# A windowed-attention and feed-forward kernel: the weight loads are begun by GpSimd's queue in place of SP's

## The chip, the cores and the metric

The kernel runs on one core of a Trainium2 chip. The metric is the device time of one execution in microseconds; the kernel before takes 941.67 us, the median of three runs (940.76 to 941.94). Engines are named as in the profile: PE (matmul), DVE (VectorE), ACT (ScalarE), POOL (GpSimd) and SP (the engine whose queue begins transfers).

## The reference

For 8 batches, 8 heads, 576 positions and 64 numbers per head, attention looks back over a window: heads 0 to 3 see the last 32 positions, heads 4 to 7 every fourth of the last 128. The heads side by side give rows of 512, which go through a norm and a feed-forward block with a residual.

```python
scores = scale * np.matmul(q, k.transpose(0, 1, 3, 2))
scores = np.where(masks[None, :, :, :], scores, -1000000000.0)
attn = np.exp(scores - np.max(scores, axis=-1, keepdims=True))
attn_out = np.matmul(attn / (np.sum(attn, axis=-1, keepdims=True) + 1e-09), v)
x = attn_out.transpose(0, 2, 1, 3).reshape(B, S, H * D)          # (8, 576, 512)
xn = (x - mean) / np.sqrt(var + 1e-06) * g_ln
out = x + np.maximum(xn @ w_ch1, 0.0) @ w_ch2                    # 512 -> 2048 -> 512
```

The two weight matrices come in as 64-bit numbers (8.4 MB each).

## The kernel before

The 4608 rows are 36 tiles of 128, taken three to a block. Each tile goes through attention (scores, softmax, values), the norm, two DMA transposes into `xT` (`transposes`, L576), the up matmuls (L597, 2048 hidden numbers in four groups of 512) and the down matmuls (L620). Every fp32 operand of the feed-forward block is held as two fp16 halves, so a product is three matmuls.

**The weights** are read once, at the start. `to_f32` (L645) loads a piece of 1 MB into a tile named `slot` (for the first column group of w1 two pieces of 0.5 MB), turns the 64-bit numbers into fp32 with one ACT operation (L659) and three DVE operations (L661, L662, L666), and lets PE sum the absolute values (L673). There are 18 such loads: four of 0.5 MB and six of 1 MB for w1 (`prep_w1`), eight of 1 MB for w2 (`load_w2`). When a whole column group of w1 is in, its scale is found (`scale_of`, L680) and the group is split into halves (`split_w1`, L153 on ACT and L154 on DVE). w2 has one scale, known only when the last load is summed; then `split_w2` splits it in eight steps, here called P0 to P7, and the down matmuls can begin, tile by tile.

**Slots.** The `slot` tiles share five buffers. They hold the weight pieces, the values of the first four tiles, the keys and queries of every second later tile, and the split keys of each tile. A load into a slot waits until the slot's previous user is done.

**Tiles 0 to 3** (`EARLY`) run in fp32 (`scores_early` and the like) between the weight loads. From tile 4 on, `load_tile_now` loads keys and queries (L186), `prep_stacked` splits them on ACT and POOL (L308, L279, L309, L280). Each group of nine tiles needs a scale for its values, found in `scale_v`: nine loads of a 256 KB row tile (L225, two buffers, shared with other tiles of that name), each squared by ACT (L226), then a sum on DVE (L228) and a matmul on PE (L230).

**What sets the order.** The pieces of work are units with a due time (`TIMES`, `MOVED`), emitted in order of that time; then the framework's scheduler places the instructions of each engine in one fixed order by its own model of their durations, and every engine and queue works its list in order. All transfers are begun by SP, so a transfer that must wait for a buffer holds up all transfers behind it. One more rule sits beside the weights: `state["raw"]` keeps the last weight load, and the loads of tiles 0 to 5 are emitted inside `tc.issue_after(raw)` (`after_weights`, L161), which puts instructions of that load's own engine behind it.

Of the kernel before, what the change touches and what calls it, by code (L numbers as in the profile page):

```python
# [68 lines left out]
def attention_then_ffn(ctx: ExitStack, tc, qkv, masks, g, w1, w2, out):  # L69
    nc = tc.nc  # L70
# [88 lines left out]
    state = {}  # L159
# [90 lines left out]
    def slot():  # L250

        return work.tile([P, CW * DM * 2], I32, name="slot", bufs=SLOTS)
# [392 lines left out]
    def to_f32(src, dst, ps, weights, start, stop, first=False):  # L645

        nw = len(weights)
        raw = slot().rearrange("p (a c two) -> p a c two", a=nw, two=2)  # L650
        src = src.rearrange("(a p) c two -> p a c two", p=P)
        step = 1 if first else nw
        for a in range(0, nw, step):
            on = slice(a, a + step)
            state["raw"] = nc.sync.dma_start(out=raw[:, on], in_=src[:, on]).ins
            lo, hi, at = raw[:, on, :, 0], raw[:, on, :, 1], dst[:, on]


            nc.scalar.activation(at, hi.bitcast(F32), AF.Abs, scale=2.0**-112)  # L659
            mi = at.bitcast(I32)  # L660
            nc.vector.tensor_scalar(mi, mi, scalar1=3, scalar2=None, op0=ALU.logical_shift_left)  # L661
            nc.vector.scalar_tensor_tensor(  # L662
                out=lo, in0=lo, scalar=29, in1=mi, op0=ALU.logical_shift_right, op1=ALU.bitwise_or
            )

            nc.vector.scalar_tensor_tensor(  # L666
                out=mi, in0=hi, scalar=SIGN_BIT, in1=lo, op0=ALU.bitwise_and, op1=ALU.bitwise_or
            )

        up = raw.bitcast(BF16).rearrange("p a c two -> p a (c two)").rearrange("p a (c four) -> p a c four", four=4)[:, :, :, 1]  # L670
        for a in range(nw):
            for c in range(0, DM, SUMS):
                nc.tensor.matmul(  # L673
                    ps[:, 0:SUMS], weights[a], up[:, a, c : c + SUMS],
                    start=start and a == 0 and c == 0, stop=stop and a == nw - 1 and c == DM - SUMS,
                )
# [13 lines left out]
    def prep_w1(fg):  # L690
        if fg == 0:
            nc.scalar.activation(g_abs, g_sb, AF.Abs)
        fs = slice(fg * DM, (fg + 1) * DM)
        wf = w1_sb[:, fg + 1]
        ps = ps_f.tile([P, DM], F32, name="ps_f")
        for c in range(0, NKC, CW):
            to_f32(
                w1[c * P : (c + CW) * P, fs], wf[:, c : c + CW], ps,
                [repeated(g_abs[:, c + a : c + a + 1]) for a in range(CW)],
                c == 0, c == NKC - CW, fg == 0,  # L700
            )
        s1.append(scale_of(ps, T_W1, f"s1_{fg}"))
# [8 lines left out]
    def load_w2(f):  # L711
        if f == 0:
            state["w2_ps"] = ps_f.tile([P, DM], F32, name="ps_f")
        to_f32(
            w2[f * P : (f + CW) * P, :], w2_f32(f, CW), state["w2_ps"], [repeated(s1[f // 4][:, 1:2])] * CW,
            f == 0, f == NFC - CW,
        )
# [195 lines left out]
```

## Time and profile before

| | |
|---|---|
| median of three runs | 941.67 us |
| profiled execution, its own time | 944.02 us |
| its span, first to last instruction | 942.2 us |
| granted TensorE clock, mean over the span | 0.985 |
| PE busy | 890.7 us |
| PE idle | 51.5 us, most of it in the first 140 us |

The profile lists, per engine, when each instruction ran, what ended the idle time before it, and when a transfer's data arrived. The span is cut into stretches below; a stretch's row gives each engine's busy time in it.

### The profile page before, as it was taken

The numbers are of one execution on the slowest core, as the hardware profiler recorded it, in microseconds if no ns is written. First come the engines' busy times: TensorE is split into PE (matmuls) and PEld (weight loads), VectorE is DVE, ScalarE is ACT, GpSimd is POOL, SyncE is SP. The second block draws the span as 40 slices with busy tenths as digits, with TensorE's granted clock in tenths as the row PEclk, the third lists the DMA queues.
The fourth block names the chain that finished last, engine by engine and source line by source line (L and its number), as shares of the span: only waits on it lengthen the run. The fifth ranks groups of instructions, "written<-read, shape, count | busy, mean of one in ns | idle before, by whom it ended". The sixth has DMA issues, their size and how long they took to land.

```text
span 942.2 us, 18610 instructions
## 1 busy us (share of the span) xinstructions
PE 890.7 (95%) x7608; PEld 552.2 (59%) x7608; DVE 634.2 (67%) x1379; ACT 312.7 (33%) x588; POOL 312.3 (33%) x319
## 2 busy tenths in 40 slices
PE   4479789999999999999999999999999999999998
PEld 4379466777665555565565565565565565564553
DVE  4799658896977577786686686686686685660210
ACT  4556742334323343251241451241241341130110
POOL 1010273646234235454253353354243341120000
PEclk9979899999999999999999999999999999999999
DMA  7887872754344516446143654364043411010000
GB/s 241 311 229 229 187 176 50 153 122 115 66 75 93 148 52 133 92 71 136 37 80 71 169 105 71 89 123 90 30 88 69 87 27 37 21 24 23 12 1 34
DMA packets 79622, 93.39 MB, mean 99 GB/s; under 512 B 47920, under 2 KB 53680, under 8 KB 79536
## 3 DMA queue, kind: packets, MB, share of 16 engines
q1 hardware_dynamic: 79536, 92.21, 42.3%
q8 instruction: 59, 0.97, 0.4%
q14 instruction: 27, 0.22, 0.1%
HBM read 71.86 MB, written 9.44 MB: 86 GB/s over the span
## 4 chain that ended last, share of the span: by engine, by line
PE 81%; DMA 10%; ACT 3%; DVE 3%; issue 2%; SPq 1%; POOL 1%; ACTq 0%; DVEq 0%; POOLq 0%
PE ps_f L597 36%; PE ps_f L620 35%; PE ps_s L330 4%; PE ps_v L528 4%; DMA row<-in_qkv 4%; DMA slot<-in_w 3%; DMA xT<-xl 1%; ACT row L226 1%; DMA slot<-in_qkv 1%; DMA v<-in_qkv 0%; PE ps_f L673 0%; ACT w_sb L153 0%; DVE slot L662 0%; POOL slot L280 0%; DVE slot L154 0%
## 5 line engine op out<-in xcount | busy, mean ns | idle before, releaser
L620 PE MATMUL ps_f<-w_sb,hh 128*128 128x512 f16 x1152 | 345.0, 380 | 5.8 <-ACT w_sb L153 5.0
L597 PEld LDWEIGHTS <-w_sb 128*128 128x128 f16 x3072 | 256.0, 99 | 126.6 <-issue 4.6
L620 PE MATMUL ps_f<-w_sb,hl 128*128 128x512 f16 x576 | 219.1, 380 | 0.0
L597 PE MATMUL ps_f<-xT,w_sb 128*128 128x384 f16 (+1 forms) x1536 | 199.2, 289 | 2.9 <-DMA xT<-xh 2.4
L597 PE MATMUL ps_f<-w_sb 128*128 128x384 f16 (+1 forms) x1536 | 196.7, 287 | 0.0
L620 PEld LDWEIGHTS <-hh 128*128 128x128 f16 x1152 | 111.8, 98 | 131.5 <-issue 6.8
L603 ACT ACTIVATE hh<-ps_f 128x384 f16<-128x384 f32 (+1 forms) x184 | 91.1, 500 | 216.8 <-PE ps_f L597 216.8
L604 DVE SCALAR_TENSOR_TENSOR hl<-ps_f,hh 128x384 f16<-128x384 f32 (+1 forms) x184 | 100.2, 569 | 42.4 <-ACT hh L603 40.3
L620 PEld LDWEIGHTS <-hl 128*128 128x128 f16 x576 | 56.5, 98 | 67.1 <-issue 1.8
L362 DVE TENSOR_TENSOR sc<-ps_s,mask 32x256 f32<-32x256 f32 x128 | 53.6, 419 | 51.2 <-PE ps_s L330 49.8
L435 DVE STREAM_TRANSPOSE pt_d<-pk 32x256 f32<-32x256 f32 x128 | 79.4, 621 | 1.8
L626 DVE SCALAR_TENSOR_TENSOR row<-ps_f,s,x 128x512 f32<-128x512 f32 x36 | 27.0, 749 | 74.5 <-PE ps_f L620 74.0
L446 POOL TENSOR_TENSOR sc<-sc,mx 128x512 f32<-128x512 f32 x32 | 33.4, 1043 | 116.3 <-DVE mx L444 116.3
L451 ACT ACTIVATE p<-sc 128x512 f32<-128x512 f32 x32 | 20.2, 631 | 128.2 <-POOL sc L446 128.2
L569 POOL TENSOR_TENSOR xl<-xn,xh 128x512 f16<-128x512 f32 x36 | 42.0, 1166 | 59.1 <-ACT xh L568 49.8
L330 PE MATMUL ps_s<-slot 128*128 128x128 f16 (+1 forms) x768 | 58.8, 226 | 2.1 <-DVE sc L348 2.1
L330 PEld LDWEIGHTS <-slot 128*128 128x128 f16 x768 | 50.9, 99 | 12.7 <-DVE sc L348 3.0
L287 POOL COPY slot<-slot 128x128 f16<-128x128 f16 x56 | 17.5, 340 | 119.4 <-PE ps_v L528 119.3
L348 DVE TENSOR_TENSOR sc<-ps_s,mask 32x256 f32<-32x256 f32 x128 | 53.5, 418 | 4.9 <-PE ps_s L330 3.4
L453 POOL TENSOR_TENSOR pk<-p,pk 128x512 f16<-128x512 f32 x32 | 40.7, 1271 | 45.8 <-ACT pk L452 45.8
L458 DVE STREAM_TRANSPOSE pt_b<-pk 32x128 f16<-32x128 f16 x87 | 26.1, 300 | 42.0 <-ACT pk L452 28.4
L554 POOL TENSOR_TENSOR rstd<-rstd,mhalf 128x1 f32<-128x1 f32 x36 | 21.1, 587 | 94.9 <-DVE rstd L553 85.2
(100 smaller groups left out, 961.3 us busy)
## 6 DMA issues: line engine op xcount, KB each, us to landing
qk<-in_qkv SPq DMA_DIRECT2D x36, 512.0 KB, 6.9
slot<-in_qkv SPq DMA_DIRECT2D x32, 512.0 KB, 6.7
slot<-in_w SPq DMA_DIRECT2D x14, 1024.0 KB, 6.3
out_x<-row SPq DMA_DIRECT2D x36, 256.0 KB, 2.0
row<-in_qkv SPq DMA_DIRECT2D x33, 256.0 KB, 2.9
v<-in_qkv SPq DMA_DIRECT2D x33, 256.0 KB, 3.0
slot<-in_w SPq DMA_DIRECT2D x4, 512.0 KB, 7.3
slot<-in_qkv SPq DMA_DIRECT2D x28, 64.0 KB, 4.5
```

The source lines that it names most:

```text
L330: nc.tensor.matmul(out, lhs, rhs, start=(n == 0), stop=(n == len(terms) - 1))
L348: nc.vector.tensor_tensor(out=sc[pj, 0:HP, :], in0=ps[pj, :, W * j : W * j + 2 * W], in1=mask_16[pj, m : m + 1, :].broadcast_to([W, HP, 2 ...
L362: nc.vector.tensor_tensor(out=sc[pj, HP:H, :].rearrange("p h (t i) -> p h t i", t=2), in0=ps[pj].rearrange("p h (t c) -> p h t c", t=2)[:, ...
L435: nc.vector.transpose(dd[pj].rearrange("p t h (i r) -> p r t h i", r=DIL)[:, j], pk[pj, HP:H, :].rearrange("p h (t i) -> p t h i", t=2),)
L446: nc.gpsimd.tensor_tensor(out=sm, in0=sc, in1=mx.broadcast_to([P, H, 2 * W]), op=ALU.subtract)
L453: nc.gpsimd.tensor_tensor(out=pk16[:, :, :, 1], in0=p32, in1=pk16[:, :, :, 0], op=ALU.subtract)
L528: nc.tensor.matmul(oo, l, r, start=(n == 0), stop=(n == len(mm) - 1))
L569: nc.gpsimd.tensor_tensor(out=xl, in0=xn, in1=xh, op=ALU.subtract)
L597: nc.tensor.matmul(z[:, n], l, r, start=(m == 0), stop=(m == len(mm) - 1))
L603: nc.scalar.activation(hh, z, AF.Relu)
L604: nc.vector.scalar_tensor_tensor(out=hl, in0=z, scalar=0.0, in1=hh, op0=ALU.max, op1=ALU.subtract)
L620: nc.tensor.matmul(o, l, r, start=(f == 0 and m == 0), stop=(f == NFC - 1 and m == 2))
```

## The change

The weight loads are begun by POOL's queue; nothing else in the text changes.

```diff
@@ -652,7 +652,7 @@
         step = 1 if first else nw
         for a in range(0, nw, step):
             on = slice(a, a + step)
-            state["raw"] = nc.sync.dma_start(out=raw[:, on], in_=src[:, on]).ins
+            state["raw"] = nc.gpsimd.dma_start(out=raw[:, on], in_=src[:, on]).ins
             lo, hi, at = raw[:, on, :, 0], raw[:, on, :, 1], dst[:, on]
```

The rule of `issue_after` names the engine of the weight load. With the load on POOL it holds back only the POOL instructions of the tile loads (memsets), and no longer SP's transfers; and the scheduler places everything anew in the first part of the program. From about the third block on the orders are the same. Three places, as the programs list them.

SP's queue at the start, the rows behind the mask's load: before, and then with the change. `in_w` are the weights, `qk_103` keys and queries of an early tile, `slot<-in_qkv` values of tiles 0 and 1, `row<-in_qkv` the rows of the values' scale, `v_1332` and `v_1428` the values of tiles 4 and 3.

```order
L655 DMA slot<-in_w 128x1024 x4
L213 DMA slot<-in_qkv 32x3x128
L213 DMA slot<-in_qkv 32x4x128 x2
L213 DMA slot<-in_qkv 32x3x128
L213 DMA slot<-in_qkv 32x4x128 x2
L175 DMA qk_103<-in_qkv 128x1024
L213 DMA slot<-in_qkv 32x4x128 x8
L655 DMA slot<-in_w 128x2x1024 x2
L225 DMA row<-in_qkv 128x512 x2
```

```order
L175 DMA qk_103<-in_qkv 128x1024
L225 DMA row<-in_qkv 128x512
L194 DMA v_1332<-in_qkv 128x512
L293 DMA v_1428<-in_qkv 128x512
L225 DMA row<-in_qkv 128x512
L213 DMA slot<-in_qkv 32x4x128 x3
L213 DMA slot<-in_qkv 32x3x128
L213 DMA slot<-in_qkv 32x4x128 x2
L213 DMA slot<-in_qkv 32x3x128
L213 DMA slot<-in_qkv 32x4x128 x7
```

The weights are gone from SP, tile 1's keys and the values of tiles 3 and 4 are loaded first of all (before, the latter came behind the last weight load), and tile 0's values come behind a row load that waits for a buffer.

POOL's queue with the change, from the first weight load to the last; before, the same rows stood there without L655. `mask_80` is the mask that tile 0's scores need, `rstd` and `xl` belong to the norms of tiles 0 and 1.

```order
L655 DMA slot<-in_w 128x1024 x4
L203 MEMSET slot 128x8x2
L655 DMA slot<-in_w 128x2x1024
L203 MEMSET slot 128x8x2
L740 CAST mask_80<-row 128x384
L655 DMA slot<-in_w 128x2x1024 x5
L203 MEMSET slot 128x8x2
L655 DMA slot<-in_w 128x2x1024
L554 TENSOR_TENSOR rstd<-rstd,mhalf 128x1
L655 DMA slot<-in_w 128x2x1024
L569 TENSOR_TENSOR xl<-xn,xh 128x512
L655 DMA slot<-in_w 128x2x1024
```

```order
L203 MEMSET slot 128x8x2
L554 TENSOR_TENSOR rstd<-rstd,mhalf 128x1
L655 DMA slot<-in_w 128x2x1024 x2
L569 TENSOR_TENSOR xl<-xn,xh 128x512
L655 DMA slot<-in_w 128x2x1024 x3
```

Five loads now stand ahead of the mask's cast, and the last seven alternate with the norms of tiles 0 and 1.

ACT's queue around the splitting of w2: before, and then with the change. `w_sb<-w_sb,s_...` are the steps P0 to P7, `row,v_sums` the squared rows, `slot<-qk_1329` the keys and queries of tile 4, `pk` the exponentials of tile 3.

```order
L413 ACTIVATE pk<-ps_s,less 128x64 x8
L603 ACTIVATE hh<-ps_f 128x4x128
L153 ACTIVATE w_sb<-w_sb,s_2_1539 128x2x512
L308 CAST slot<-qk_1329 128x1024
L279 CAST slot<-qk_1329 128x4x128
L279 CAST slot<-qk_1329 128x512
L226 ACTIVATE row,v_sums<-row 128x512 x2
L153 ACTIVATE w_sb<-w_sb,s_2_1539 128x2x512
L153 ACTIVATE w_sb<-w_sb,s_3_1541 128x2x512
```

```order
L413 ACTIVATE pk<-ps_s,less 128x64 x8
L153 ACTIVATE w_sb<-w_sb,s_0_1535 128x2x512 x2
L226 ACTIVATE row,v_sums<-row 128x512
L561 ACTIVATE xn<-x,shift,rstd 128x512
L603 ACTIVATE hh<-ps_f 128x4x128
L423 COPY pt_a_81<-ps_s 128x256
L425 COPY pt_d_85<-ps_s 128x64 x4
L308 CAST slot<-qk_1329 128x1024
L279 CAST slot<-qk_1329 128x4x128
L279 CAST slot<-qk_1329 128x512
L226 ACTIVATE row,v_sums<-row 128x512
L153 ACTIVATE w_sb<-w_sb,s_1_1537 128x2x512
```

Before, five of the eight steps stand ahead of tile 4's keys; now only P0 and P1 do. On PE the order follows: ahead of the matmul L230 that closes the scale for tiles 9 to 17, the program before has 72 down matmuls (L620), 19 up matmuls of block 1 (L597) and 8 score matmuls of tile 4 (L330); with the change 54, none and 24. Ahead of the first L620, both have 384 L597.

## Rows read from the trace of the kernel before

**Rows 1.** The page: the span, the engines' busy time, and the 40 equal slices (23.6 us each) with PE's busy tenths.

```profile
span 942.2 us, 18610 instructions
PE 890.7 (95%) x7608; PEld 552.2 (59%) x7608; DVE 634.2 (67%) x1379; ACT 312.7 (33%) x588; POOL 312.3 (33%) x319
...
PE   4479789999999999999999999999999999999998
```

**Rows 2.** Busy time of each engine (and count of instructions) in stretches of 20 us, then granted clock, DMA share and GB/s.

```profile
0.00:20.00 20.00, 7.74 (x128) 6.19 (x130) 8.22 (x20) 7.26 (x20) 3.93 (x20) 1.00 0.74 217
20.00:40.00 20.00, 9.30 (x159) 8.06 (x159) 14.08 (x23) 9.00 (x16) 0.12 (x1) 1.00 0.97 360
40.00:60.00 20.00, 11.76 (x110) 10.54 (x110) 17.84 (x34) 14.19 (x31) 3.51 (x3) 0.77 0.90 240
60.00:80.00 20.00, 19.23 (x345) 18.48 (x344) 19.99 (x35) 10.46 (x14) 2.16 (x2) 0.89 0.87 225
80.00:100.00 20.00, 18.84 (x382) 18.17 (x380) 17.68 (x39) 12.90 (x31) 1.71 (x2) 1.00 0.53 190
100.00:120.00 20.00, 15.39 (x66) 7.09 (x66) 10.88 (x11) 16.19 (x34) 7.23 (x5) 0.83 0.94 201
120.00:140.00 20.00, 15.39 (x208) 13.00 (x206) 10.01 (x27) 10.11 (x22) 13.40 (x15) 0.91 0.72 168
```

**Rows 3.** The weight loads as a group (line L655): ns that SP spends on one issue (least, median, most) with the first and last start, and us from issue to landing.

```profile
L655 SPq DMA_DIRECT2D slot<-in_w x18: 368/390/942, 2.1 to 82.7; - x18
...
DMA to landing us min/median/max: 4.8/6.8/13.2
```

**Rows 4.** Waits of SP's own queue between 0 and 150 us: total us, times, longest.

```profile
SPq L225 <- ACT row L226: 15.7, 10, 6.6
SPq L213 <- DMA slot<-in_w: 11.1, 7, 3.3
```

**Rows 5.** The timeline of 0 to 40 us: start, us, engine, line; in brackets the idle time before it and what ended it.

```profile
2.12 1.87 SPq L655 DMA_DIRECT2D slot<-in_w  x4
...
2.93 0.97 POOL L202 MEMSET slot<- 128x1040 f32 x1
...
8.62 0.66 ACT L659 ACTIVATE w_sb<-slot 128x512 f32<-128x512 f32 x1 [6.01 <-DMA slot<-in_w]
...
17.69 1.51 SPq L655 DMA_DIRECT2D slot<-in_w  x2
...
23.24 1.12 ACT L659 ACTIVATE w_sb<-slot 128x1024 f32<-128x1024 f32 x1 [1.21 <-DMA slot<-in_w]
...
28.74 0.90 SPq L655 DMA_DIRECT2D slot<-in_w  x2
...
38.79 1.12 ACT L659 ACTIVATE w_sb<-slot 128x1024 f32<-128x1024 f32 x1 [6.59 <-DMA slot<-in_w]
...
39.95 0.69 DVE L661 TENSOR_SCALAR w_sb<-w_sb 128x1024 int32<-128x1024 int32 x1 [3.48 <-ACT w_sb L659]
```

**Rows 6.** The timeline where tile 0's norm ends and the first up matmuls begin.

```profile
50.08 1.47 POOL L569 TENSOR_TENSOR xl<-xn,xh 128x512 f16<-128x512 f32 x1 [7.69 <-ACT xh L568]
...
58.75 5.17 PE L597 MATMUL ps_f<-xT,w_sb 128*128 128x128 f16 x47 [0.18 <-DMA xT<-xl]
```

**Rows 7.** The timeline of the last weight loads and of SP behind them.

```profile
78.05 4.97 SPq L655 DMA_DIRECT2D slot<-in_w  x2
...
85.56 1.13 ACT L659 ACTIVATE w_sb<-slot 128x1024 f32<-128x1024 f32 x1 [1.65 <-DMA slot<-in_w]
...
89.94 1.17 ACT L659 ACTIVATE w_sb<-slot 128x1024 f32<-128x1024 f32 x1
...
91.75 3.16 SPq L247 DMA_DIRECT2D v_b<-vh  x4
...
96.70 0.89 SPq L225 DMA_DIRECT2D row<-in_qkv  x2
```

**Rows 8.** The timeline from the first step of w2's splitting to L230.

```profile
102.69 2.17 ACT L153 ACTIVATE w_sb<-w_sb,s 128x1024 f16<-128x1024 f32 x2
...
103.24 1.41 SPq L186 DMA_DIRECT2D qk<-in_qkv  x2
...
112.68 1.05 ACT L308 CAST slot<-qk 128x1024 f16<-128x1024 f32 x1 [0.16 <-DMA qk<-in_qkv]
...
130.35 0.63 ACT L226 ACTIVATE row<-row 128x512 f32<-128x512 f32 x1 [5.28 <-DMA row<-in_qkv]
...
132.51 0.54 PE L230 MATMUL ps_v<-v_tot,ones 128*128 128x1 f32 x2 [4.61 <-DVE x L486]
```

**Rows 9.** Pieces of the chain that ended last: start, us, what; they give the pace of PE's matmuls at full clock.

```profile
134.14 1.80 PE ps_s L330 x16
135.94 2.75 PE ps_f L597 x48
...
146.55 7.77 PE ps_f L620 x36
```

**Rows 10.** Groups of instructions between 0 and 100 us by shape: busy us, mean ns of one; then the idle time before them.

```profile
L662 DVE SCALAR_TENSOR_TENSOR slot<-slot,w_sb 128x1024 int32<-128x1024 int32 x14 | 18.4, 1317 | 0.1
...
L661 DVE TENSOR_SCALAR w_sb<-w_sb 128x1024 int32<-128x1024 int32 x14 | 9.6, 686 | 9.1 <-ACT w_sb L659 9.1
```

**Rows 11.** One POOL operation over the widest operand of the early stage, from the timeline.

```profile
121.17 2.13 POOL L309 TENSOR_TENSOR slot<-slot 64x1024 f16<-64x1024 f32 x1 [0.34 <-ACT slot L308]
```

## The prediction

> **What bounds the kernel now.** I read the page first [rows 1]: PE is busy 890.7 of 942.2 us, and in the 40 slices it is full from the sixth on. So the end moves only with PE's idle time, 51.5 us in all. The stretches of 20 us [rows 2] say where that lies: 12.3 + 10.7 + 8.2 = 31.2 us before 60 us, 0.8 + 1.2 from 60 to 100, and 4.6 + 4.6 from 100 to 140; only 9 us come later. The change touches the loads of the first 90 us, so the question is when PE gets its first up matmuls (58.75 [rows 6]), when its down matmuls begin (the first step of w2's split, 102.69), and when L230 is passed (132.51 [rows 8]). Behind that point the orders soon agree and PE is full, so a shift there goes through to the end.
>
> Next I read who holds up the weights. In SP's queue, row loads wait 15.7 us for ACT's squares and value loads 11.1 us for transfers [rows 4], and whatever waits there holds the next weight. DMA is nearly full at the same time (0.97 of the engines from 20 to 40 us, 360 GB/s [rows 2]), so bytes can be moved earlier only where the queue left a hole.
>
> **The change, part by part.** Times are against the profiled execution (span 942.2, its own time 944.02, so 1.8 around it); the median of the three runs is 941.67, and I put the difference on that.
>
> *Removed from SP:* 18 issues of 0.39 us [rows 3], 7.0 us. SP is never the bound of such a small sum; only the waits it hands on count.
>
> *Added to POOL:* 18 issues. No row shows POOL issuing a transfer. From below it could cost SP's 0.39 [rows 3], from above a wide POOL operation, 2.13 [rows 11]; I take 1.0, near the memset of a whole slot, 0.97 [rows 5]. From issue to landing I keep 6.8, with 4.8 and 13.2 as the ends [rows 3].
>
> *Term 1, the first up matmuls.* POOL begins only when its memsets end, at 2.93 + 0.97 = 3.90 [rows 5], against 2.12. By the time the fourth piece lands, SP's 2.0 MB of other loads and 2.1 MB of weights have passed; at 360 GB/s that is 11.4 us, from about 3: 14.4 to 15.5. The first piece comes at 3.9 + 6.5 (8.62 - 2.12 [rows 5]) = 10.4 in place of 8.6. So about 2 us are lost here. The fifth load, issued now at 17.69 behind tile 1's values and landed at 23.24 [rows 5], can go at 8; by bytes (6.3 MB at 360 GB/s) it lands near 20, and 3 us are won. From there each load goes as soon as its slot is free, not when SP comes to it: the load issued at 28.74 and landed at 38.79, after which DVE had been idle 3.48 [rows 5], should be issued near 27 and land at 27 + 6.8 = 34. The 3.48 vanish; 1 us is lost at the front of DVE's list, where tile 0's scores wait for a mask that POOL casts after five issues. Net -2.5: xl of tile 0 at 47.6 in place of 50.08, first up matmuls at 56.2 in place of 58.75 [rows 6]. Bounds: -5, when the earlier fifth load counts in full as well, and +3, when a slot's turn costs POOL's 2.13 and the early 2 us are never made up.
>
> *Term 2, the down matmuls.* From 60 to 100 us PE is busy 38.1 of 40 [rows 2]; earlier weights can't shorten that, they only move it: -2.5. Now the split starts at 102.69, because ACT stands at a row's square until the row lands. With the change two more squares and tile 3's exponentials stand ahead of P0, but the rows are asked for earlier (below), so I put P0 at about 100. This gives PE little: P0 and P1 feed a quarter of each tile's down matmuls, and P2 now stands behind tile 4's keys.
>
> *Term 3, tile 4's keys and L230.* The keys are issued at 103.24 and reach ACT at 112.68 [rows 8]. Ahead of them SP does v_b (91.75) and the first rows (96.70) [rows 7]. v_b waits for values of tiles 3 and 4 that are loaded behind the last weight issue, and for an ACT list with the last load's L659 (89.94) in it. Changed: those values are in since the start, their scale no longer waits for the next-to-last load, and the conversion stands ahead of the last L659. With everything 2.5 to 3 earlier I get: next-to-last load issued at 75.2 in place of 78.05, + 1.0 + 6.5 landed at 82.7 (85.56 [rows 7]); L659 to 83.9, values converted at 84.6, v_b from then on, first rows 4 us later at 88.4. Rows land after some 3.3, two squares and the next pair land and are squared at 97.8; keys issued at 98.3, 4.9 earlier. Their transit is 9.4 now; tile 2's transposes, which ran beside it, now come behind, so I take 8.5: ACT has them at 106.8, 5.9 earlier.
>
> From the keys to L230 are 19.8 us now (132.51 - 112.68). With the change the same list stands between, the row that closes the scale again lands 17.7 us after the keys (130.35 - 112.68 [rows 8]), but tile 3's DVE work is done by then: about 18.8. Against this, PE has 18 down and 19 up matmuls still to do and 16 score matmuls already done: 18 x 0.216 + 19 x 0.057 - 16 x 0.11 = 3.9 + 1.1 - 1.8 = 3.2 us [rows 9]. So PE is as far as now at 106.8 + 18.8 + 3.2 = 128.8 in place of 132.51.
>
> **Sum:** -3.7 us. That is a span of 938.5, a profiled time of 940.3, and for the timed median 941.67 - 3.7 = 938.0. Term 1 is contained in term 3's chain and not added.
>
> **The rivals.**
>
> *No gain at the front.* xl of tile 0 stands on POOL behind a load that waits for a slot. For it: 7.69 us of POOL's idle there ended with ACT [rows 6], and a load ahead of it could end later. Against it: that slot's user is done on DVE near 46 by term 1. Then terms 1 and 2 are nothing, the keys come at 112.68 - 5.9 + 2.5 = 109.3, and PE is as far as now at 131.3; with the transit at 9.4, at 132.2. Time 940.5 to 941.4. Here the Trainium skill speaks too ("DMA: Bandwidth & Descriptors", section "Issuing engines are not separate DMA queues"): transfers of all issuing engines run on the same 16 DMA engines, and several issuers save only issue time. By it the whole gain is the 7.0 us of SP's time, which no one waits for, and the time 941.7. The DMA share of 0.97 agrees with it; the waits of rows 4 are what it leaves out.
>
> *Slower: POOL's path from free slot to landed data is long.* The loads of w2 reuse their slots in turn, and the last two each wait for the one three before. If every turn costs more than my 1.0 + 6.5, the keys' chain has three such turns in it (first load, middle, next to last). My sum is gone when the keys come at 106.8 + 3.7 = 110.5, that is at 1.2 us more a turn; at 3 us more a turn the keys come at 115.8, and the time is 941.67 - 3.7 + 9 = 947.0. For it: the longest of SP's loads took 13.2 [rows 3], and POOL's issue price is unknown. Against it: DVE is the fuller engine from 40 to 80 us (37.8 of 40 [rows 2]), and hides part.
>
> *Descriptors starved by DVE.* L661 takes 686 ns for the same 1024 columns for which L662 takes 1317 [rows 10], so it runs in a faster mode. One L661 goes with each load; if POOL's issue has to wait for one at each of the three turns, 3 x 0.69 = 2.1 us come off: 938.0 + 2.1 = 940.1. The Trainium skill has the rule ("SBUF — State Buffer", section "SBUF: two separate sides"): while DVE runs in a mode with two ports, GpSimd can't write its descriptors. No run here shows it yet.
>
> **How the numbers follow.** A measurement here tells 0.2%, 1.9 us, from no change: 939.8 to 943.6. The forecast has 0.5, no gain 0.17, the slow path 0.25, starved descriptors 0.08. The forecast's own range (-8 to 0: keys' transit 7 to 9.4, front -5 to 0) lies mostly under 939.8, 0.45 of its 0.5; with a little from the others: faster 0.47, same 0.22, slower 0.31. For 8 in 10 the range goes down to a front of -5 with keys 9 earlier, 932.5, and up to the slow path at 3 us a turn, 947.5.
>
> **What would show it.** Right: first up matmuls near 56, DVE with no gap of 3 us before 40, the first step of w2's split near 100, tile 4's keys on ACT near 107, L230 near 126, PE idle after 100 us no more than now. Wrong: loads that land more than 8 us after their slot is free, POOL idle in front of the norm with a load ahead of it, or keys after 110.5.

## The result, and the profile after

With the change the kernel takes 947.25 us (median of 4 runs, 947.16 to 950.66); before, on the same chip, 941.81 (4 runs, 940.76 to 943.78). The ratio is 1.0064, interval 1.0036 to 1.0092: 0.6% slower, where 938.0 was predicted. The profiled execution took 950.66 (span 948.9), that of before 944.02 (span 942.2 [rows 1]); they lie 3.4 and 2.2 us above their medians.

The page of the changed kernel (span, busy time of the engines, PE's tenths in 40 slices):

```profile
span 948.9 us, 18636 instructions
PE 891.7 (94%) x7608; PEld 552.1 (58%) x7608; DVE 636.0 (67%) x1379; ACT 312.5 (33%) x588; POOL 327.4 (35%) x337
...
PE   2489779999999989999999999999999999999998
```

PE's work is the same, its idle time is 57.2 us in place of 51.5: that is 5.7 of the 6.7 us between the spans, and the rest is PE's busy time, 1.0. The stretches of 20 us, columns as in [rows 2] (busy time of PE, PEld, DVE, ACT, POOL; granted clock, DMA share, GB/s):

```profile
0.00:20.00 20.00, 5.18 (x87) 4.07 (x88) 8.06 (x19) 7.25 (x18) 7.69 (x27) 1.00 0.94 299
20.00:40.00 20.00, 11.53 (x199) 9.98 (x199) 12.76 (x20) 9.80 (x20) 2.74 (x5) 1.00 0.93 296
40.00:60.00 20.00, 11.16 (x103) 10.13 (x103) 20.00 (x41) 13.30 (x29) 5.46 (x6) 1.00 0.77 209
60.00:80.00 20.00, 17.24 (x284) 16.90 (x284) 18.11 (x33) 9.21 (x14) 4.04 (x5) 0.83 0.81 251
...
100.00:120.00 20.00, 15.28 (x148) 10.04 (x146) 10.51 (x24) 15.88 (x37) 7.19 (x6) 0.91 0.97 223
120.00:140.00 20.00, 14.89 (x105) 7.99 (x104) 13.19 (x24) 11.16 (x18) 18.02 (x15) 0.91 0.77 155
140.00:160.00 20.00, 17.64 (x210) 13.06 (x208) 13.57 (x29) 3.52 (x6) 3.59 (x3) 1.00 0.26 60
```

Before 60 us PE is idle 32.1 us, where the prediction saw a gain on 31.2. DMA, 0.74 full in the first 20 us before, is now at 0.94. Behind that PE is idle 2.8 us in 60 to 80 (0.8 before), 0.2 in 80 to 100 (1.2), 9.8 in 100 to 140 (9.2) and 3.9 in 140 to 180 (1.6).

The clock of 1.00 that these rows and [rows 2] give for the first stretches is not PE's speed there: the trace holds no clock record that early. Eight matmuls of one kind (L420) of before, at 44 us and at 87 us, both in stretches with 1.00:

```profile
44.10:46.30 2.20, 2.13 (x11) 2.07 (x12) 2.20 (x6) 2.20 (x7) 0.00 (x0) 1.00 0.44 106
44.17 2.08 PE L420 MATMUL ps_s<-ident,pk 128*128 128x128 f32 x8 [1.07 <-ACT pk L413]
86.63 1.11 PE L420 MATMUL ps_s<-ident,pk 128*128 128x128 f32 x8
```

In e14 (below) the same eight take 2.08 us at 44.41, with a recorded clock of 0.50, the lower level of 1.2 GHz. So PE runs at the lower level through its first stretches, before and with the change alike.

The weight loads themselves, as in [rows 3] (ns of POOL for one issue; us from issue to landing):

```profile
L655 POOL DMA_DIRECT2D slot<-in_w x18: 527/713/898, 3.8 to 84.7; - x18
...
DMA to landing us min/median/max: 5.3/7.2/14.0
```

So POOL's issue costs 0.71 us and a load lands after 7.2: neither is slow. What has become slow is what SP still loads. The first values (L213, those of 6 to 30 us, least, median, most us from issue to landing), before:

```profile
DMA to landing us min/median/max: 2.9/4.1/9.4
```

and with the change:

```profile
DMA to landing us min/median/max: 6.5/9.4/10.0
```

The reason stands in the DMA queues of the first 60 us (packets, MB, share of 16 engines' time). Before:

```profile
q1 hardware_dynamic: 8720, 16.29, 86.6%
```

With the change (q0 is POOL's queue):

```profile
q0 software_dynamic: 2752, 10.49, 49.6%
q1 hardware_dynamic: 6064, 5.54, 38.1%
```

86.6% before, 87.7% after: with the second queue the engines moved no more than with one. What the weights get earlier, SP's small transfers get later. The last four rows of the first scale show who pays (timeline of ACT, DVE and SP):

```profile
22.30 11.92 SPq L225 DMA_DIRECT2D row<-in_qkv x4
...
31.53 0.63 ACT L226 ACTIVATE row<-row 128x512 f32<-128x512 f32 x1 [7.00 <-DMA row<-in_qkv]
...
32.16 1.10 ACT L659 ACTIVATE w_sb<-slot 128x1024 f32<-128x1024 f32 x1
...
33.29 0.69 DVE L661 TENSOR_SCALAR w_sb<-w_sb 128x1024 int32<-128x1024 int32 x1 [6.21 <-ACT w_sb L659]
```

The first two of them land 9.1 and 9.3 us after their issue, the other two after 5.6 and 4.6. (The six rows of before took 7.4, 7.4, 2.8, 3.0, 10.4 and 10.7, so rows as such are not slower; the third of them landed at 30.53 before and lands at 31.43 now.) The weight that L659 converts at 32.16, the sixth, had landed at 25.69, but in ACT's new list the third row's square stands ahead of it, so ACT idles 7.00 us and DVE 6.21; before, that square stood behind the seventh weight. The 3.48 us of DVE [rows 5] that the prediction wanted back have become 6.21. Then xl and the first up matmuls, to be laid beside [rows 6]:

```profile
51.27 0.82 POOL L655 DMA_DIRECT2D slot<-in_w  x1 [3.52 <-ACT xn L561]
52.81 1.42 POOL L569 TENSOR_TENSOR xl<-xn,xh 128x512 f16<-128x512 f32 x1 [0.72 <-ACT xh L568]
...
59.35 3.63 PE L597 MATMUL ps_f<-xT,w_sb 128*128 128x128 f16 x48
```

The first group starts 0.6 us later than before and ends 0.9 us earlier (62.98 for 63.92), since PE comes to full speed during it, and before only at its end. The loss begins behind it:

```profile
72.00 1.09 PE L673 MATMUL ps_f<-slot,s 128*128 128x128 bf16 x8 [2.76 <-DVE slot L662]
72.92 6.25 PE L597 MATMUL ps_f<-xT,w_sb 128*128 128x128 f16 x65
...
82.12 0.71 POOL L655 DMA_DIRECT2D slot<-in_w  x1 [6.72 <-PE ps_v L230]
...
71.30:78.00 6.70, 6.00 (x56) 6.00 (x56) 6.67 (x8) 3.65 (x5) 2.02 (x2) 0.50 0.89 299
```

PE stands 2.76 us for a weight piece, the granted clock falls to 0.50, and the 65 up matmuls take 6.25 us (3.7 at the pace of [rows 9]). Behind them in PE's list stands the sum of a piece of w2 (L673, done at 81.57), and only then is that piece's slot free for the next-to-last load (the row names L230, which PE ran next): begun at 82.12 and landed at 88.03, where before it was begun at 78.05 and landed at 85.54. The last one lands at 92.02 (88.51).

And the later stations, beside [rows 8]:

```profile
103.04 1.41 SPq L186 DMA_DIRECT2D qk<-in_qkv  x2
...
105.50 2.23 ACT L153 ACTIVATE w_sb<-w_sb,s 128x1024 f16<-128x1024 f32 x2
...
112.06 1.05 ACT L308 CAST slot<-qk 128x1024 f16<-128x1024 f32 x1 [1.77 <-DMA qk<-in_qkv]
...
131.54 0.38 PE L230 MATMUL ps_v<-v_tot,ones 128*128 128x1 f32 x2 [1.89 <-DVE v_tot L228]
...
142.41 1.07 PE L330 MATMUL ps_s<-slot 128*128 128x128 f16 x16 [1.27 <-DVE sc L348]
...
148.14 2.84 PE L597 MATMUL ps_f<-xT,w_sb 128*128 128x128 f16 x48 [0.86 <-DVE hl L604]
...
160.15 0.19 PE L528 MATMUL ps_v<-vh,pt_a 128*128 128x65 f16 x1
```

L230 comes 1.0 us earlier, but PE's list was re-ordered too and less work lies before it. Tile 4's value matmuls (L528) start at 160.15, in the trace of before at 154.16: 6.0 of the 6.7 us between the spans are there by then.

```profile
154.16 0.19 PE L528 MATMUL ps_v<-vh,pt_a 128*128 128x65 f16 x1
```

### The profile page after: what moved, and what is told of

Its sections match the earlier page's. It is cut to its first block, busy times and chain, and to the rows that moved or that the text cites. A ratio compares the mean times of both kernels' runs of the same rounds, so it can differ in the third digit from the quotient of the medians.

```text
span 948.9 us, 18636 instructions
## 1 busy us (share of the span) xinstructions
PE 891.7 (94%) x7608; PEld 552.1 (58%) x7608; DVE 636.0 (67%) x1379; ACT 312.5 (33%) x588; POOL 327.4 (35%) x337
## 4 chain that ended last, share of the span: by engine, by line
PE 78%; DMA 5%; DVE 4%; POOL 2%; ACT 2%; issue 1%; SPq 1%; ACTq 0%; POOLq 0%; DVEq 0%
PE ps_f L620 35%; PE ps_f L597 35%; PE ps_v L528 4%; PE ps_s L330 4%; DMA row<-in_qkv 3%; POOL slot L280 1%; DMA qk<-in_qkv 1%; DVE pt_d L435 1%; DMA v<-in_qkv 1%; ACT row L226 1%; POOL slot L309 1%; PE ps_f L673 0%; DVE slot L662 0%; DVE pt_a L432 0%; ACT vh L153 0%
## 5 line engine op out<-in xcount | busy, mean ns | idle before, releaser
L620 PE MATMUL ps_f<-w_sb,hh 128*128 128x512 f16 x1152 | 345.9, 381 | 3.0 <-DVE w_sb L154 1.7
L597 PEld LDWEIGHTS <-w_sb 128*128 128x128 f16 x3072 | 256.4, 99 | 124.6 <-issue 3.2
L620 PE MATMUL ps_f<-w_sb,hl 128*128 128x512 f16 x576 | 218.9, 380 | 0.0
L597 PE MATMUL ps_f<-xT,w_sb 128*128 128x384 f16 (+1 forms) x1536 | 198.7, 290 | 1.1 <-DVE hl L604 1.1
L597 PE MATMUL ps_f<-w_sb 128*128 128x384 f16 (+1 forms) x1536 | 196.7, 287 | 0.0
L620 PEld LDWEIGHTS <-hh 128*128 128x128 f16 x1152 | 112.0, 98 | 127.6 <-issue 3.8
L604 DVE SCALAR_TENSOR_TENSOR hl<-ps_f,hh 128x384 f16<-128x384 f32 (+1 forms) x184 | 100.1, 569 | 47.7 <-ACT hh L603 45.8
L620 PEld LDWEIGHTS <-hl 128*128 128x128 f16 x576 | 56.5, 98 | 68.0 <-issue 3.1
L330 PE MATMUL ps_s<-slot 128*128 128x128 f16 (+1 forms) x768 | 58.1, 224 | 4.9 <-DVE sc L348 3.9
L330 PEld LDWEIGHTS <-slot 128*128 128x128 f16 x768 | 50.2, 98 | 16.7 <-DVE sc L348 5.2
L348 DVE TENSOR_TENSOR sc<-ps_s,mask 32x256 f32<-32x256 f32 x128 | 53.5, 418 | 4.9 <-PE ps_s L330 3.4
```

Source lines behind the costliest of these rows:

```text
L330: nc.tensor.matmul(out, lhs, rhs, start=(n == 0), stop=(n == len(terms) - 1))
L348: nc.vector.tensor_tensor(out=sc[pj, 0:HP, :], in0=ps[pj, :, W * j : W * j + 2 * W], in1=mask_16[pj, m : m + 1, :].broadcast_to([W, HP, 2 ...
L597: nc.tensor.matmul(z[:, n], l, r, start=(m == 0), stop=(m == len(mm) - 1))
L604: nc.vector.scalar_tensor_tensor(out=hl, in0=z, scalar=0.0, in1=hh, op0=ALU.max, op1=ALU.subtract)
L620: nc.tensor.matmul(o, l, r, start=(f == 0 and m == 0), stop=(f == NFC - 1 and m == 2))
```

## The experiments

The theories. **Displacement**: the loads on GpSimd's queue start earlier on DMA engines that are full, SP's small transfers land later, and ACT and DVE wait for them in list order. **Order**: the queue is harmless, and the new order of all engines (or the lost tie of `after_weights()`, L161, which holds SP's tile loads behind the weights) costs the time. **POOL's list**: loads and norms hold each other up on POOL.

To part queue from order, I pinned the order of each engine at the start of the kernel by dependencies without a semaphore, from a table of instruction numbers at the kernel's end. In the pinned kernels `after_weights()` does nothing, since the table holds the order. In the table 974, 977, 980, 983, 986, 989 are the six row loads, 975 to 990 their squares, 992 their sum. Ratios are to the kernel before on the same chip. The stations, each from one profiled execution (us; U0 the first full group of tile 0's up matmuls, P0 the first step of w2's split, V4 tile 4's first L528), and PE's idle time before 60 and from 60 to 140 us:

| kernel | ratio (interval) | U0 | P0 | V4 | idle 0-60 | 60-140 |
|---|---|---|---|---|---|---|
| before | 1 | 58.75 | 102.69 | 154.16 | 31.2 | 11.2 |
| the change | 1.0064 (1.0036-1.0092) | 59.35 | 105.50 | 160.15 | 32.1 | 12.8 |
| e1 queue only | 1.0084 (1.0062-1.0107) | 57.64 | 105.15 | 157.44 | 30.3 | 14.0 |
| e4 tie only | 0.998 (0.9959-1.0) | 52.56 | 103.13 | 151.29 | 24.9 | 12.8 |
| e5 rows later, new order | 1.0027 (1.0006-1.0049) | 54.64 | 100.18 | 155.02 | 27.6 | 14.8 |
| e6 rows later, old order | 0.9998 (0.9974-1.0022) | 54.20 | 102.05 | 154.11 | 26.5 | 13.5 |
| e7 as e6, weights on SP | 0.9993 (0.9974-1.0013) | 52.58 | 98.93 | 152.62 | 24.9 | 12.7 |
| e12 rows later still | 1.0009 (0.9995-1.0024) | 51.67 | 101.64 | 153.95 | 24.5 | 14.7 |
| e14 loads held | 1.0050 (1.0033-1.0067) | 56.92 | 105.21 | 156.87 | 31.7 | 12.9 |

Single executions of one kernel differ by some us (e6's twelve runs lie between 937.08 and 945.41), so the stations say where time goes and the ratios how much. The ratios are those on record with their intervals; the medians quoted give slightly other ones (e1: 1.0069).

**e1, the queue alone**: the order of before on every engine, the 18 loads on GpSimd.

```diff
-            state["raw"] = nc.sync.dma_start(out=raw[:, on], in_=src[:, on]).ins
+            state["raw"] = nc.gpsimd.dma_start(out=raw[:, on], in_=src[:, on]).ins
```

> The 18 weight loads are issued by GpSimd as in the change, but PE, ACT, DVE, SP and GpSimd's own computations are kept in the order that they had in the kernel before (the loads stand among GpSimd's computations where the scheduler puts them). Order theory (the change lost because every engine was put in a new order in the first 150 us): 937 to 941.5 us, load 1b converted before 26 us and no idle DVE of 6 us at 27 to 33 us. Queue theory (GpSimd's own queue delays the loads, by its computations and by 0.7 to 0.9 us for one issue): 945 to 949 us, with loads that land over 8 us after their slot came free.

Measured 948.96 against 942.45. The queue alone costs as much as the whole change; order as the cause fell. ACT's timeline in e1:

```profile
24.75 1.13 ACT L659 ACTIVATE w_sb<-slot 128x1024 f32<-128x1024 f32 x1 [1.86 <-DMA slot<-in_w]
30.45 0.63 ACT L226 ACTIVATE row<-row 128x512 f32<-128x512 f32 x1 [4.57 <-DMA row<-in_qkv]
...
32.63 0.63 ACT L226 ACTIVATE row<-row 128x512 f32<-128x512 f32 x1 [1.46 <-DMA row<-in_qkv]
...
33.26 1.10 ACT L659 ACTIVATE w_sb<-slot 128x1024 f32<-128x1024 f32 x1
38.25 0.63 ACT L226 ACTIVATE row<-row 128x512 f32<-128x512 f32 x1 [3.89 <-DMA row<-in_qkv]
...
40.95 2.13 ACT L659 ACTIVATE w_sb<-slot 128x1024 f32<-128x1024 f32 x2
```

The weight converted at 40.95 had landed at 32.88, 6 us before the one of [rows 5] (L659 at 38.79, on landing), and is converted 2 us later: the first two rows land 9.8 and 11.4 us after issue (7.4 before), the next two 7.0 and 6.9 (2.8 and 3.0), and they stand ahead. U0 is 1 us early all the same. So e1's loss lies behind 60 us: PE waits 3.0 us for tile 1's transposes (0.6 before), 3.7 for P0 (5.0) and 4.8 for L230 (4.6).

**e2, the order alone**: the orders of the change, the weights on SP.

```diff
-            state["raw"] = nc.gpsimd.dma_start(out=raw[:, on], in_=src[:, on]).ins
+            state["raw"] = nc.sync.dma_start(out=raw[:, on], in_=src[:, on]).ins
```

> The weights are issued by SP as before, but PE, ACT, DVE, GpSimd and SP's other transfers stand in the order of the changed kernel, with the weight loads merged into SP's list by the scheduler. Order theory: 945 to 950 us, since the row that ACT waits for at 24 to 31 us still stands behind 14 loads of values on SP. Queue theory: 940 to 943 us, since no load stands behind a computation of GpSimd.

951.32, ratio 1.0103 (1.0084 to 1.0123), above both ranges. This tells little: ACT's new list begins with a row that on SP stands behind nine other transfers, five of them weights, ACT waits 14.88 us for it, and PE is busy 1.47 us in the first 20. The new order presupposes the second queue.

**e3, the rows' squares one weight later**, in the change's order:

```diff
-    "117 975 121 126 140 978 145 215-222 301 202 204 206 208 228-232 981 315 984 467 987 481 990 531 339 "
+    "117 975 121 126 140 978 145 215-222 301 202 204 206 208 228-232 315 981 467 984 481 987 990 531 339 "
```

> The changed kernel with all engines held in its own order, but on ACT the squares of three rows of values (of tiles 5 to 7) each stand one weight piece later and the fourth right behind them, so that no weight piece of w1 waits for a row. Order theory, with the row as the main stall: the idle 6.2 us of DVE at 27 to 33 us is gone, the first matmul of the up projection comes at 54 to 57 us in place of 59.35, and the time is 941 to 945 us. Queue theory: the next load takes the place of the row and the time is 946 to 948.5 us.

950.51, ratio 1.0101 (1.0075 to 1.0127), a miss. DVE's gap of 6.21 is gone (L661 at 27.80), but the sum of the rows (L228) now waits 4.05 us for ACT at 41.50, in DVE's list ahead of tile 0's norm, and the first up matmuls start at 59.55. The wait had moved one place along the same list.

**e4, the tie alone**: the kernel before, weights on SP, nothing pinned.

```diff
-        return nullcontext() if raw is None else tc.issue_after(raw)
+        return nullcontext()
```

> The kernel before, weights on SP, with the tie alone taken away that holds the loads of tiles 0 to 5 behind the last weight load on SP; the scheduler makes its own order of it. Order theory: the tie is what the change lost, so 943 to 949 us. Queue theory: 940.5 to 942.5 us, no change that can be told.

940.2 against 942.45: the lost tie costs nothing.

**e5 and e6, rows out of the way**: the last four rows (e5, new order) or all six (e6, old order) are loaded, squared and summed behind the first tile's norm. The loads of weights stay on GpSimd. SP's list in e6:

```diff
-    "102 104 115 108-113 272 275-282 974 977 980 983 986 989 565 568-575 335-336 899-906 516-517 896 1333 "
+    "102 104 115 108-113 272 275-282 565 568-575 974 977 335-336 980 983 899-906 986 989 516-517 896 1333 "
```

> The changed kernel in its own order, but the last four rows of values are loaded, squared and summed only after the norm of tile 0 (SP's loads behind the values and the transposes of tile 0, ACT's squares at 50 us and later, DVE's sum of them behind tile 1's norm), so that no weight piece and no norm waits for a row. Theory of the shared engines (what SP issues lands later because the 1 MB loads of a second queue share the DMA engines with it, and ACT and DVE wait in their order for what landed late): no idle DVE of over 3 us between 27 and 50 us, the first up matmul at 54 to 57 us, 942 to 946 us. Theory of GpSimd's own queue (the weight loads themselves come late, behind GpSimd's computations): 946.5 us or more.

> All engines in the order of the kernel before, weights on GpSimd, and all six rows moved behind the norm of tile 0 in the same way. Theory of the shared engines: the pieces of w1, which landed up to 6 us earlier than on SP, are now also converted earlier, first up matmul at 53 to 56 us, and 940 to 945 us, under the 949 of the same order with the rows in their old place. Theory of GpSimd's own queue: 946 to 949 us as before the move.

e5 944.98 and e6 941.78 against 942.87. With the rows gone from between the weights, the cost of the queue falls from 0.84% to nothing in the old order, from 0.64% to 0.27% in the new one. ACT's timeline in e6 has the weights as they land:

```profile
28.59 1.17 ACT L659 ACTIVATE w_sb<-slot 128x1024 f32<-128x1024 f32 x1 [2.53 <-DMA slot<-in_w]
31.19 1.14 ACT L659 ACTIVATE w_sb<-slot 128x1024 f32<-128x1024 f32 x1 [1.43 <-DMA slot<-in_w]
35.26 1.14 ACT L659 ACTIVATE w_sb<-slot 128x1024 f32<-128x1024 f32 x1 [2.93 <-DMA slot<-in_w]
```

In e1 the last two of these ran from 40.95. This is the front that Term 1 had in mind.

**e7, the control**: e6's lists, the weights on SP.

```diff
-            state["raw"] = nc.gpsimd.dma_start(out=raw[:, on], in_=src[:, on]).ins
+            state["raw"] = nc.sync.dma_start(out=raw[:, on], in_=src[:, on]).ins
```

> The control: the kernel before with the weights on SP and the six rows moved in the same way. Both theories: 940 to 943 us, no change that can be told, since there the rows landed before they were needed. Were it clearly faster, the rows would be a cost of their own and the comparison with the weights on GpSimd has to be made against this run.

943.01 against 942.87. Moving the rows gains nothing where the weights are on SP, so e6 did not offset a loss by an unrelated gain: what e6 took away is the queue's cost, which needs the rows between the weights. The control shows a second thing. U0 is 6.2 us early, P0 3.8, V4 1.5, and the time is unchanged. Where the front's gain goes stands in PE's waits between 60 and 140 us (us in total, times, longest). Before:

```profile
PE ps_f L620 <- ACT w_sb L153: 5.0, 1, 5.0
PE ps_v L230 <- DVE x L486: 4.6, 1, 4.6
...
PE ps_f L597 <- DMA xT<-xh: 0.6, 1, 0.6
```

in e6:

```profile
PE ps_f L620 <- ACT w_sb L153: 5.7, 1, 5.7
PE ps_v L230 <- DVE x L486: 2.9, 1, 2.9
PE ps_f L673 <- DVE slot L662: 2.4, 2, 2.1
PE ps_f L597 <- DMA xT<-xh: 1.5, 1, 1.5
```

PE comes earlier and waits longer: for tile 1's transposes, for the bound of w2 (L673) and for P0.

**e8 and e9, half of the loads**: w2's 8 (e8) or w1's 10 (e9) on GpSimd, the order of before.

```diff
+            state["raw"] = (nc.gpsimd if ("w2_ps" in state) is True else nc.sync).dma_start(out=raw[:, on], in_=src[:, on]).ins
```

(that is e8; e9 has `is False`.)

> The order of the kernel before; the ten loads of w1 stay on SP in their old place, and only the eight of w2 are issued by GpSimd. If the loss of the queue lies in the first 45 us (rows and values behind w1): 940.5 to 943 us. If it lies behind 60 us (tile 1's transposes behind a w2 load, and loads behind GpSimd's norm): 944 to 947 us.

> The order of the kernel before; the ten loads of w1 are issued by GpSimd, the eight of w2 by SP in their old place. Theory of the shared engines, with the rows and values behind w1 as its main cost: most of what the whole move costs in this order, 945 to 949 us, with rows that land 9 us or more after their issue and ACT idle for them between 25 and 41 us. Theory of GpSimd's own queue (loads held by the norms, of which only w2's loads have one ahead of them): 941 to 943.5 us.

944.59 against 942.87, ratio 1.0023 (1.0004 to 1.0042), and 944.16 against 942.37, 1.0021 (1.0005 to 1.0037). Each half costs 0.2%, both together 0.84: the parts don't add up. e9 missed the range of displacement: values land after 9.1 us (median of 14) and the first two rows after 10.6 and 12.2, as late as in e1, and yet it loses a quarter of what e1 loses. Late small transfers at the front are not most of the cost.

**e10, another second queue**: all loads issued by ACT, the order of before.

```diff
+            state["raw"] = nc.scalar.dma_start(out=raw[:, on], in_=src[:, on]).ins
```

> The order of the kernel before, with all 18 weight loads issued by ACT in place of GpSimd, where the scheduler puts them. Theory of the shared engines: any second queue does it, so the values of tile 1 and the rows land 8 us or more after their issue, and 945 to 950 us. Theory of GpSimd's own queue (its slower issue, its computations): 940 to 944 us, with values and rows as late as before at most.

949.23, ratio 1.0069 (1.0049 to 1.009): the expected time by another way. The values land in 3.7 us (median), and U0 comes at 60.79. The reason is in the semaphores that the trace names. Each SP transfer carries one of eight, taken in turn, and waits until the transfer eight places before it has landed. POOL's loads have eight of their own, so in the change they are in flight beside SP's; ACT's loads share SP's eight. In e10 the sixth load therefore waits for a value of SP, which landed at 21.52, and ACT's list stands with it:

```profile
22.11 0.37 ACT L423 COPY pt_a<-ps_s 128x256 f32<-128x256 f32 x1 [5.76 <-DMA slot<-in_qkv]
```

So e10 does not test displacement: a second queue with no more transfers in flight did not delay the values. That the number in flight is what does it agrees with this, but no run varied it alone.

**e11, the rows on GpSimd**, weights on SP:

```diff
-            nc.sync.dma_start(out=vs, in_=qkv[t, :, NQK:])
+            nc.gpsimd.dma_start(out=vs, in_=qkv[t, :, NQK:])
```

> The other way round: weights on SP as in the kernel before and its order kept, but the rows (0.25 MB each) are issued by GpSimd. Theory of the shared engines: small loads on the second queue hold the large ones up little, rows land no later than before, 940 to 943 us. Theory of GpSimd's own queue: rows come behind its computations, ACT and the split of w2 wait for them, 944 us or more.

954.86, ratio 1.0135 (1.0113 to 1.0158), the slowest of all, though U0 (54.85) and P0 (98.93) are early. The loss lies behind: PE is busy 27.65 us from 100 to 140 (30.79 before), and ACT waits 3.4, 3.0, 2.8 and 4.1 us there for rows (13.4 us in all from 60 to 140, 7.0 before), which now stand in POOL's list among its computations; PE waits 10.1 us for L230 (4.6 before).

**e12, rows later still** than in e6:

```diff
-    "102 104 115 108-113 272 275-282 565 568-575 974 977 335-336 980 983 899-906 986 989 516-517 896 1333 "
+    "102 104 115 108-113 272 275-282 565 568-575 335-336 974 977 899-906 980 983 986 989 516-517 896 1333 "
```

> As the run with the order of the kernel before, weights on GpSimd and the rows moved behind tile 0's norm, but with the rows squared only from 60 us on and their sum after tile 1's norm, so that no weight piece waits for a row at 44 to 52 us either. If the front's gain reaches the end: first up matmul at 52 to 54.5 us, first step of the split of w2 at 98 to 101 us (102.69 before), 937 to 941 us. If it is given back behind 100 us: the same two times, and yet 941 to 944 us.

943.18 against 942.37. U0 is 7.1 us early, P0 1.1, V4 0.2, the time not at all.

**e13 and e14, what stays behind 60 us.** e13 is e1 with two swaps in POOL's list (load 945 ahead of tile 1's rstd 507, and xl 297 ahead of load 708); e14 is e1 with three early loads held behind operations of ACT, so that SP's small transfers go first:

```diff
+    for load, first in HOLDS:
+        tc.add_manual_dep(by[f"I-{load}"], f"I-{first}", mybir.DependencyInfo(mybir.DependencyClass.Sync, mybir.DependencyReason.DATA), reason="hold")
+HOLDS = ((300, 228), (466, 202), (480, 978))
```

> The run with the order of the kernel before and all weight loads on GpSimd (949 us), with two swaps in GpSimd's list alone: the fifth w2 load stands ahead of tile 1's power of the variance in place of behind it, and tile 0's low half of x ahead of the second w2 load in place of behind it. Theory of GpSimd's own queue as the second part of the loss: the fifth w2 load issued at 68 to 69 us (70.04), tile 1's transposes landed by 79.5 us (80.60 and 81.08), 944 to 947 us. Theory of the shared engines alone: the transposes still land behind a w2 load, 948 to 950 us.

> The run with the order of the kernel before and all weight loads on GpSimd (949 us; rows in their old place), but three loads of w1 wait until about the moment at which SP issued them before: the fifth for ACT's first copy of tile 0's transposed weights (17.65 us), the seventh for the first split of w1 (20 us), the eighth for the second row's square (28 us). Theory of the shared engines (the early loads of the second queue displaced the values and rows): values of tile 1 land in some 4 us again, the first two rows by 28 us, and 941 to 945 us, though weights are held back. Theory of GpSimd's own queue: later loads only cost more, 948 to 951 us.

e13: 947.74, ratio 1.0057 (1.0038 to 1.0077). e14: 947.18, 1.0050 (1.0033 to 1.0067). Both times lie between the ranges of the two theories. In e14 the rows land at 20.81 and 22.21 (30.43 and 32.55 in e1), as displacement wanted, so displacement at the front can be undone by starting loads later; about 0.3% comes back, with intervals that overlap. Some 0.5% stays: PE waits 2.42 us for tile 1's transposes; the first line is of before, the second of e14:

```profile
78.40 3.25 PE L597 MATMUL ps_f<-xT,w_sb 128*128 128x128 f16 x50 [0.65 <-DMA xT<-xh]
78.48 5.76 PE L597 MATMUL ps_f<-xT,w_sb 128*128 128x128 f16 x50 [2.42 <-DMA xT<-xh]
```

They start as before, since PE came to the wait earlier, but take 2.5 us longer. The stretch around them in e14 (columns as in [rows 2]) shows why, a granted clock of 0.50:

```profile
78.40:84.20 5.80, 5.63 (x52) 5.47 (x53) 4.10 (x8) 0.58 (x2) 0.00 (x0) 0.50 0.90 340
```

The 2.5 us reach the split of w2: the last load waits for a slot that PE's sum (L673) frees, in PE's list behind these 50 matmuls, so it is begun at 85.70 (82.65 before) and lands at 90.97 (88.51), and P0 comes at 105.21 (102.69). In e1 the same matmuls start 2.2 us late and run at 0.50 for part of their time, and the last load lands at 92.42. This is read from one execution of each. e13 doesn't tell whether it is POOL's list or the w2 loads ahead of the transposes: e6 has loads and transposes in the same queues and lost nothing.

**What the losing kernels share.** In the profiled executions of the change, e1, e2, e3, e10, e13 and e14, all with ratios of 1.005 or more, the last w2 load lands at 90.6 to 92.4 us and P0 comes at 105.0 to 106.1. In before, e4 to e9 and e12, with ratios up to 1.0027, it lands at 85.2 to 88.9 and P0 comes at 98.9 to 103.1. Only e11 loses in another place. So the larger part of the loss goes with late last loads of w2, for which the whole of the split waits. No run delayed them alone.

## Why the prediction was wrong

*What bounds the kernel*: right. The loss is PE's idle time, and most of it is there by V4.

*The price of an issue on POOL*, 1.0 us with bounds 0.39 and 2.13: measured 0.71 (0.53 to 0.90). *Issue to landing*, 6.8: measured 7.2. Neither was at fault.

*Term 1, the first up matmuls at 56.2*: this step failed. They came at 59.35. Its landings came true: the fifth load at 20.17 (forecast 20), the one of 28.74 issued at 27.07 and landed at 34.66 (27 and 34); but ACT converted that one only at 38.56, as before. It took each weight's earlier landing as gain, and costed the work behind it, SP's values and rows, at the landing times of before. The number that spoke against it was read, DMA at 0.97 in 20 to 40 us [rows 2], and was used only for the weights' bytes. Weights did land earlier; values went from 4.1 to 9.4 us, the rows for which ACT waits took 9.1 and 9.3, and ACT and DVE take them in list order. e1 (queue alone, 1.0084), e6 (rows gone, 0.9998) and its control e7 (0.9993) show that queue and rows together cost the time; e9 and e14 show that the late transfers alone are the smaller part of it. The bytes gave no warning, since what became late is small: the four rows are 1 MB of the 16 moved by 60 us.

*Terms 2 and 3, P0 at about 100 and tile 4's keys at 106.8*: P0 came at 105.50, the keys at 112.06. The step that failed here, and that carried the forecast of the time, is the next-to-last load, put at 75.2 and landed at 82.7: it was begun at 82.12 and landed at 88.03, for the wait, the clock and the order on PE that the result shows. The "first rows at 88.4" became 94.36, the keys' issue 103.04 in place of 98.3. Besides, "earlier weights only move it: -2.5" fails by itself too. In e6, e7 and e12 the front is 4.6 to 7.1 us early and P0 0.6 to 3.8, V4 0.1 to 1.5, the time within its interval of none. The next in-order waits (tile 1's transposes, w2's bound, P0, L230) take the gain. Ahead of the keys SP waits mostly for ACT's cast of values (L247 for L153: 9.4 us until 89.84, 2.1 until 97.37), and that cast (89.11) stands behind the conversion of the next-to-last load.

*L230 near 126, PE no more idle after 100 us than now*: L230 at 131.54; 9.8 us idle in 100 to 140 and 3.9 in 140 to 180 (9.2 and 1.6 before). The term for the score matmuls was misread besides: the 1.80 us for 16 of [rows 9] lie in a stretch with a granted clock of 0.50 (134.1 to 135.9 us), and at full clock 16 take 1.07 (142.41 above), so 0.7 us less come off. In the re-ordered list PE waits for L348 and L604 at 142 and 148, where the prediction took the orders to have met.

*The rivals.* "No gain at the front" named a place: xl (52.81) stands on POOL behind a load that waits for its slot until 51.27. But that issue was over at 52.09, and xl waited for ACT's xh; it gave 941.4 at most. The slow path gave 947.0, near the time, and with it the upper end of the range holds the result; that is luck, since its cause was another: from issue to landing POOL's loads are not slow. Its sign, keys after 110.5, came true for the slot's wait behind PE. Starved descriptors: a small sign only. In ten kernels with loads on POOL, the 14 issues that ran beside an L661 for 0.4 us or more took 0.82 us (median; longest 1.75), the 112 others after the first 6 us 0.72; in the change that makes 0.4 us in all, not 2.1. No rival had SP's transfers in it. The Trainium skill's rule ("DMA: Bandwidth & Descriptors", section "Issuing engines are not separate DMA queues") is borne out in its first half (all issuers share the 16 engines) by the shares of the two queues, 49.6 + 38.1 against 86.6; by its second half, that only issue time is saved, the time would have been 941.7, and the 947.25 differ. The Trainium skill says on the same page (section "SWDGE vs HWDGE vs iDMA") that each DMA engine round-robins between the queues that the two kinds of issuer feed; the doubled landing time of SP's values agrees with it, but no run here shows the turn-taking itself.

*What stays open.* How e1's loss behind 60 us divides between the transposes, POOL's list and PE's clock, and whether the clock falls there in every execution (in e14's profile it is 2.5 us); what delays the last loads of w2 in e2, e3 and e10; why the halves of e8 and e9 don't add up; and what the new order is worth with the second queue (e1 to the change: 0.2% less, intervals overlap; e6 to e5: 0.3% more). No version was clearly faster than before; e4 is nearest, its interval ending at 1.0.

## What to carry to other kernels

Before bulk loads get a queue of their own, look at the share of the DMA engines in that stretch: where they are full, an earlier start for one transfer is a later landing for another, so ask which small transfers run beside it and which engine waits for those in list order, and how many transfers the program then has in flight. Then follow the gain to the next in-order wait: here 5 to 7 us at the first matmuls became less than 2 us at tile 4 and nothing at the end.

## What the runs showed of the hardware

- SP had at most eight transfers in flight: its ninth issue came 0.02 us after the landing of the one eight before, again and again (with the change 15.29 behind 15.27, 16.97 behind 16.95, 19.30 behind 19.28; before 8.62 behind 8.60, 13.38 behind 13.36). The wait is one of the program, for the semaphore that the two share; a limit of the chip is not shown. With it, slower landings also delay SP's later issues.
- A load of 0.5 or 1 MB costs POOL 0.53 to 0.90 us for the issue, SP 0.37 to 0.94 [rows 3]. Where the load waited for PE's L673, POOL's issue started 0.55 us behind it (82.12 behind 81.57; e14 85.70 behind 85.15), SP's 0.08 (before 82.65 behind 82.57).
- After PE had stood for 2.42 us (e14, 76 to 78.4) the granted clock was 0.50, TensorE's lower level of 1.2 GHz, and the next 50 up matmuls took 5.76 us, 3.25 before, where PE had stood 0.65. With the change it stood 2.76 us ahead of 72.00, and the clock was 0.50 from 71.3 to 78.0. Such a wait can cost more than its length. Where the trace has no clock record yet, the rows read 1.00 and PE's pace is that of 0.50 (with the change 16 up matmuls in 1.84 us from 59.35, in a stretch that reads 1.00).
